# Two more blocks of h, dg and du loaded through transposing DMAs, gram's sums copied out by ScalarE, and shift_k's gradient stored unturned

## The chip, the cores and the metric

The kernel runs on one core of a Trainium2 chip. The core has five engines, each with its own queue of instructions that run in order: TensorE (PE in the profile, its weight loads shown apart as PEld), VectorE (DVE), ScalarE (ACT), GpSimd (POOL), and SyncE (SP), which here does nothing but issue DMAs. Engines wait for one another on semaphores. [...] Sixteen DMA engines, fed by rings that are filled from the queues of SP and ScalarE, carry everything between HBM and SBUF. The metric is device time in microseconds (us), the median over runs.

## The reference

The computation is the forward pass and all gradients of a sum of two branches on a layernormed input. S = 2048 rows, D = 512 channels, F = 1376 hidden units, all in bf16.

```
xn = layernorm(q)
A:  k_shift = causal convolution of k with shift_k (4 taps per channel)
    kv  = k_shift * v
    y   = causal convolution of kv with ssm_k over all S rows (by FFT) + kv * ssm_D
    out_A = xn * y
B:  h = (xn @ w_gate) * (xn @ w_up);  out_B = h @ w_down
out = q + out_A + out_B
outputs: out, and the gradients of q, k, v, shift_k, ssm_k, ssm_D, w_gate, w_up, w_down
```

The gradients that matter below: those of w_gate, w_up and w_down are products over all 2048 rows, xn^T dg, xn^T du and h^T grad_out, for which h, dg and du must lie with rows on partitions. The gradient of shift_k, 512 x 4 numbers, is for each channel and tap a sum over rows of k (shifted) times the gradient of k_shift.

## The kernel before, in words

The work has three stages. In the first (to about 117 us) the layernorm, the tables of the FFT and the first transforms are done. In the second (to about 300 us) the loop over eight chunks of 256 rows computes the gate, up and down products with hidden units on partitions, multiplies them to h, dg and du, and writes the first seven chunks of those to HBM (HDD); between them the groups of the FFT are worked off. The eighth chunk's h, dg, du stay in SBUF (hd).

The third stage (from 300 us to the end) is where the change lies. Its backbone is `dw`, a loop over the 11 blocks of 128 hidden units (the last has 96). For block fb it runs `down_grad` (16 products, line L1026, into pd: the gradient of w_down) and then 64 products (L1062, into pu: the gradients of w_gate and w_up, in two halves). Both need block fb's h, dg and du with rows on partitions, and there are two ways to get them:

- Blocks 0 to 6: `load_hb` loads the block as it lies (hb, one plain DMA of 1344 KB, L793), and `hid_t` turns it on TensorE, 16 transposes for each of h, dg and du (L859, into pt); ScalarE copies each set of 16 out of PSUM (128x2048, the helper line L235). h and dg are turned before the previous block's L1062 products, du in the middle of the previous block's `down_grad`.
- Blocks 7 to 10 (`TURNED`): `load_t` loads them with a DMA that transposes on the way (natT, L817), and only the eighth chunk, which is in SBUF, is turned on TensorE by `last_t` (six transposes, L829). Block 9 (`SPLIT`) is loaded into two tiles by two DMAs, of five chunks and of two.

The buffers are few: `hb` and `natd` have two each, `nath` one. So the load for block fb + 2 waits until TensorE is through with an older block. `behind(fb)` puts some transposing loads behind a named DMA in SP's order.

Beside the backbone, generators are called at fixed steps of the loop (`sides`): `inv_y` (inverse transforms, four row groups; loads vb and kb, multiplies on VectorE into dks at L962 and kb at L963, at last loads khC), `ew` (alternating `final` and `bwd`, the elementwise work on VectorE: `final` waits for a load bb of 512 KB, L1127, at its line L1139, and needs an output buffer that an earlier output DMA must have left, L1138), `dsk_gram` and `inv_dk` (products po, L1001; outputs o5t).

`dsk_gram` makes shift_k's gradient: for each of four groups of 128 channels 32 products of dks with khC (L1085, into the PSUM tile pk), of which only the diagonal of each 64x64 square is wanted. VectorE multiplies pk by the identity straight out of PSUM (L1091, two 64x256 instructions) and sums along the row (L1093). At the end a cast to bf16 (L1096), four transposes on TensorE (L1101) and a copy out of PSUM by VectorE (dskt) turn the result so that it is stored in rows of 1 KB (L1104). ssm_D's gradient dDt is likewise turned and copied out by VectorE (L1019).

A scheduler sets the order of each engine's queue from the order of the program and its own estimates; `tc.high_priority` pulls instructions forward, `tc.issue_after` holds one behind another in its queue. SP's DMAs go out strictly in order, so a DMA that waits for its data, its buffer or a lane holds back all behind it.

Of the kernel before, what the change touches and what calls it, by code (L numbers as in the profile page):

```python
# [8 lines left out]
BF = mybir.dt.bfloat16  # L9
F32 = mybir.dt.float32  # L10
I32 = mybir.dt.int32
ALU = mybir.AluOpType
ACTF = mybir.ActivationFunctionType
AX = mybir.AxisListType
# [6 lines left out]
R = 16  # L21
P = 128
NC4 = 4
FBLK = [(i * 128, min(128, F - i * 128)) for i in range((F + 127) // 128)]
NFB = len(FBLK)
NCH = 8
SOON = 300
# [163 lines left out]
def kernel(  # L191
# [24 lines left out]
    nc = tc.nc  # L216
# [6 lines left out]
    k_n = nat(A_k[0])  # L223
# [10 lines left out]
    def act(o, i):  # L234
        nc.scalar.copy(o, i)  # L235

    def dve(o, i):
        nc.vector.tensor_copy(o, i)  # L238
# [16 lines left out]
    def P1(name, shape, dt=F32):  # L255
        return ps1.tile(shape, dt, name=name, tag="p1")

    ident = const.tile([P, P], BF, name="ident")
# [397 lines left out]
    first = ExitStack()  # L656
# [122 lines left out]
    CP = {}  # L779
# [8 lines left out]
    LG = {}  # L788
# [6 lines left out]

    hbs = {}

    TURNED = range(NFB - 4, NFB)

    def behind(fb):  # L800
        first = {NFB - 2: lambda: LG["bb"], NFB - 1: lambda: LG["og"]}.get(fb)
        return tc.issue_after(first().ins) if first else ExitStack()

    def load_t(fb):
# [14 lines left out]
            for c in range(a, e):  # L819
                nats[fb, 0][c] = t[:, c - a]  # L820

    SPLIT = NFB - 2

    def last_t(fb):
        f0, fw = FBLK[fb]
        pt = P2("pt7", [P, 3, 2, P], BF)
        for t in range(3):
            for h in range(2):
                nc.tensor.transpose(pt[:, t, h, :fw], hds[1][:fw, fb, t, h * 128:h * 128 + 128], ident[:fw, :fw])  # L829
        n7 = c2b.tile([P, 3, 2, P], BF, name="nat7", tag="dd")  # L830
        act(n7[:, :, :, :fw], pt[:, :, :, :fw])
        nats[fb, 1] = n7

    def nat_h(fb, r):
        f0, fw = FBLK[fb]
        if fb not in TURNED:
            return nats[fb, 0][:, r, :fw]
        return nats[fb, 0][r // 2][:, 0, r % 2, :] if r < R - 2 else nats[fb, 1][:, 0, r % 2, :fw]

    def nat_d(fb, r):  # L840
        f0, fw = FBLK[fb]
        if fb not in TURNED:
            return nats[fb, 1][:, :, r, :fw]
        return nats[fb, 0][r // 2][:, 1:3, r % 2, :] if r < R - 2 else nats[fb, 1][:, 1:3, r % 2, :fw]

    def hid_t(fb, t):
        if fb in TURNED:
            return
# [68 lines left out]
    c2b = ctx.enter_context(tc.tile_pool(name="c2b", bufs=2, side="right", reuse_waits="tile"))  # L917
    c2 = ctx.enter_context(tc.tile_pool(name="c2", bufs=1, side="right", reuse_waits="tile"))
# [7 lines left out]
    dsk = c2.tile([P, NC4, 4], F32, name="dsk")  # L926
# [15 lines left out]
    DKS = {}  # L942
# [70 lines left out]
    def put_dD(o5t):  # L1013
        act(dDs[:], o5t[:, :, 0, 0])
        yield
        pt = P1("ptd", [P, P], BF)
        nc.tensor.transpose(pt[:NC4, :], dDs[:], ident[:])
        dDt = c2.tile([NC4, P], BF, name="dDt")
        dve(dDt[:], pt[:NC4, :])  # L1019
        nc.sync.dma_start(out_6.rearrange("(c p) -> c p", p=128), dDt[:])  # L1020

    def down_grad(fb):
# [18 lines left out]
    def load_h(fb):  # L1041
        (load_t if fb in TURNED else load_hb)(fb)

# [35 lines left out]
    def dsk_gram():  # L1079
        for c in range(NC4):  # L1080
            pk = P2("pk", [P, 2, D])
            for r in range(R):
                for h in range(2):
                    c0 = c * 128 + 64 * h
                    nc.tensor.matmul(pk[64 * h:64 * h + 64, h, 0:256], lhsT=dks[:, r, c0:c0 + 64],  # L1085
                                     rhs=KH[0][:, r:r + 4, c0:c0 + 64], start=(r == 0), stop=(r == R - 1))
            kd = c2b.tile([P, 4, 64], F32, name="kd", tag="dd")
            with tc.high_priority(offset=SOON):
                for h in range(2):
                    hs = slice(64 * h, 64 * h + 64)  # L1090
                    nc.vector.tensor_tensor(kd[hs], pk[hs, h, 0:256].rearrange("q (j c) -> q j c", j=4),  # L1091
                                            ident[hs, hs].unsqueeze(1).to_broadcast((64, 4, 64)), op=ALU.mult)
                nc.vector.tensor_reduce(dsk[:, c, :], kd[:], axis=AX.X, op=ALU.add)  # L1093
            yield
        dskb = c2.tile([P, 4, NC4], BF, name="dskb")
        nc.vector.tensor_copy(dskb[:], dsk[:].rearrange("q c i -> q i c"))  # L1096
        for _ in range(2):
            yield
        pt = P1("pts", [P, 4, P], BF)
        for j in range(4):  # L1100
            nc.tensor.transpose(pt[:NC4, j, :], dskb[:, 3 - j, :], ident[:])  # L1101
        dskt = c2b.tile([NC4, P, 4], BF, name="dskt", tag="dd")
        dve(dskt[:], pt[:NC4].rearrange("c j q -> c q j"))
        nc.sync.dma_start(out_4.rearrange("(c p) j -> c p j", p=128), dskt[:])  # L1104
        yield

    def bwd(b):
# [15 lines left out]
    late = []  # L1123
# [35 lines left out]
    def load_kh():  # L1159
        khC = c2.tile([P, R + 3, D], BF, name="khC", tag="o5k")  # L1160
        nc.gpsimd.memset(khC[0:1, 0:3, :], 0.0)
        with tc.issue_after(LG["g"].ins):
            nc.sync.dma_start(khC[:, 3:3 + R, :], k_n)
            nc.sync.dma_start(khC[1:113, 0:3, :], k_n[0:112, R - 3:R, :])
            nc.sync.dma_start(khC[113:128, 0:3, :], k_n[112:127, R - 3:R, :])
        KH.append(khC)

    def every(gen, start, step):
# [8 lines left out]

    def put_late():
        for dst, t in late:
            nc.sync.dma_start(dst, t[:])  # L1180
        late.clear()

    def ew():
# [55 lines left out]
```

## Time and profile before

| | |
|---|---|
| median of 3 runs | 480.36 us (480.18 to 481.91) |
| the profiled execution | 481.82 us, of which span 480.0 us |
| TensorE busy | 464.5 us, 97% |
| VectorE busy | 340.5 us, 71% (80.57 of the last 97 us) |
| ScalarE busy | 305.6 us, 64% (33.02 of the last 97 us) |
| DMA | 139.85 MB, mean 291 GB/s; 96% of the rings' time in the last 97 us |

A timeline row reads: start in us from the span's start, length in us, engine, line, operation, output <- inputs, shapes, count, and in brackets the idle time of that engine just before, with what ended it. "SPq" is the DMA-issuing queue of SP. Matmuls are pipelined, so the length of a row of several runs a little beyond the start of the next; start to start is the time that they take on TensorE. In the DMA view the figures after "x1" of an issue are its size and the time from issue to landing; its slices are fortieths of the window asked for.

### The profile page before, as it was taken

What the parts mean: (1) busy time and instruction counts of PE and PEld (TensorE: products, weight loads), DVE (VectorE), ACT (ScalarE), POOL (GpSimd) and SP (SyncE); (2) the same over time, 40 slices, a digit from 0 to 9 for tenths busy, and PEclk for the clock granted to TensorE, in tenths of its full rate; (3) what the DMA queues carried; (4) which work ended last, traced back from release to release, by engine and by line L of the source; (5) the groups of instructions that cost most, each with busy time, mean ns of one, the idle gap of its engine ahead of it and who ended that gap; (6) DMA issues with size and microseconds to landing.
All of it is one profiled execution on the core that took longest, in us unless ns stands there. A gap on an engine that the chain in (4) does not pass through costs nothing.

```text
span 480.0 us, 10366 instructions
## 1 busy us (share of the span) xinstructions
PE 464.5 (97%) x4252; PEld 311.6 (65%) x4293; DVE 340.5 (71%) x609; ACT 305.6 (64%) x349; POOL 14.0 (3%) x30
## 2 busy tenths in 40 slices
PE   7999999999999999999999999999999999999996
PEld 6867755547648447447447743576777687677885
DVE  7889989979366567686777877022257899599893
ACT  4957677659568678779779975375576535233141
POOL 8000000000000000000000000110000000000000
PEclk9999999999999999999999999999999999999999
DMA  8999999989998968968978379999899979999858
GB/s 268 374 381 366 310 296 320 315 300 328 318 288 270 277 202 255 285 200 245 298 235 259 118 272 331 388 329 313 312 361 364 371 260 320 318 267 239 252 155 294
DMA packets 111132, 139.85 MB, mean 291 GB/s; under 512 B 38859, under 2 KB 84336, under 8 KB 109550
## 3 DMA queue, kind: packets, MB, share of 16 engines
q1 hardware_dynamic: 109502, 137.85, 89.7%
q10 hardware_dynamic: 1584, 1.36, 1.0%
q8 instruction: 33, 0.54, 0.5%
q14 instruction: 13, 0.11, 0.1%
HBM read 67.08 MB, written 63.41 MB: 272 GB/s over the span
## 4 chain that ended last, share of the span: by engine, by line
PE 67%; DMA 15%; DVE 14%; issue 2%; SPq 2%; ACT 1%; DVEq 0%; ACTq 0%
PE px L555 15%; PE pgu L512 13%; PE pu L1062 8%; PE py L548 7%; PE pdh L518 6%; PE pd L1026 4%; PE ps L584 3%; DMA khC<-in_A_k_dram 3%; PE pg L613 3%; DMA ssk<-in_A_ssm_k_dram 2%; PE pf L370 2%; PE pt L859 2%; DMA vb<-in_A_v_dram 2%; DMA kb<-KS 2%; DMA x_b<-in_A_q_dram 2%
## 5 line engine op out<-in xcount | busy, mean ns | idle before, releaser
L555 PE MATMUL px<-WT,hd 128*128 128x512 bf16 (+1 forms) x340 | 78.6, 379 | 1.6 <-issue 1.4
L1062 PEld LDWEIGHTS <-xnC 128*128 128x128 bf16 x704 | 67.0, 98 | 8.4 <-issue 0.6
L555 PEld LDWEIGHTS <-hd 128*128 128x128 bf16 (+1 forms) x352 | 32.8, 98 | 44.4 <-issue 7.7
L235 ACT CAST gu<-pgu 128x1024 bf16<-128x1024 f32 (+1 forms) x48 | 45.4, 946 | 16.9 <-PE pgu L512 16.7
L235 ACT CAST GO<-pg 128x1024 bf16<-128x1024 f32 x48 | 46.2, 1015 | 13.8 <-issue 7.2
L235 ACT CAST SP<-ps 128x1024 bf16<-128x1024 f32 x47 | 45.5, 1025 | 13.7 <-PE ps L584 11.8
L512 PE MATMUL pgu<-xt,Wu 128*128 128x256 bf16 (+1 forms) x352 | 53.1, 273 | 1.1 <-DVE kn L238 0.6
L600 DVE TENSOR_TENSOR T<-SP 128x2048 bf16<-128x2048 bf16 x24 | 29.3, 1222 | 34.8 <-ACT SP L235 34.7
L512 PE MATMUL pgu<-xt,Wg 128*128 128x256 bf16 (+1 forms) x352 | 52.8, 273 | 0.0
L1062 PE MATMUL pu<-natd,xnC 128*128 128x256 bf16 x448 | 51.2, 273 | 0.0
L518 PE MATMUL pdh<-gt,WdT 128*128 128x256 bf16 (+1 forms) x352 | 46.9, 273 | 0.1
L235 ACT CAST fst<-pf 128x1024 bf16<-128x1024 f32 x44 | 42.7, 1031 | 5.5 <-issue 2.3
L512 PEld LDWEIGHTS <-Wu 128*128 128x128 bf16 (+1 forms) x352 | 33.0, 100 | 15.6 <-issue 10.7
L548 PE MATMUL py<-Wd,hd 128*128 128x512 bf16 (+1 forms) x167 | 40.2, 379 | 0.8 <-issue 0.5
L235 ACT CAST og<-pu 128x1024 bf16<-128x1024 f32 (+1 forms) x11 | 10.9, 993 | 43.7 <-PE pu L1062 28.3
L518 PEld LDWEIGHTS <-WdT 128*128 128x128 bf16 (+1 forms) x352 | 34.9, 100 | 4.8
L512 PEld LDWEIGHTS <-Wg 128*128 128x128 bf16 (+1 forms) x352 | 34.8, 100 | 3.7
L235 ACT COPY natd<-pt 128x2048 bf16<-128x2048 bf16 x14 | 26.2, 1875 | 12.0 <-PE pt L859 12.0
L533 DVE TENSOR_TENSOR hd<-gu,dh 128x1024 bf16<-128x1024 bf16 (+1 forms) x48 | 30.8, 641 | 0.8
L532 DVE TENSOR_TENSOR hd<-gu 128x512 bf16<-128x512 bf16 (+1 forms) x48 | 19.0, 397 | 16.7 <-ACT gu L235 16.7
L548 PEld LDWEIGHTS <-hd 128*128 128x128 bf16 (+1 forms) x176 | 16.5, 98 | 20.8 <-issue 3.1
L600 DVE TENSOR_TENSOR U<-SP 128x2048 bf16<-128x2048 bf16 x24 | 29.2, 1218 | 0.0
(177 smaller groups left out, 687.4 us busy)
## 6 DMA issues: line engine op xcount, KB each, us to landing
HDD<-hd SPq DMA_DIRECT2D x35, 384.0 KB, 4.5
FD<-fst SPq DMA_DIRECT2D x24, 512.0 KB, 4.9
X<-FD SPq DMA_DIRECT2D x24, 512.0 KB, 5.5
GD<-GO SPq DMA_DIRECT2D x24, 512.0 KB, 3.9
g<-GD SPq DMA_DIRECT2D x11, 1024.0 KB, 8.9
hb<-HDD SPq DMA_DIRECT2D x7, 1344.0 KB, 10.2
bb<-BX SPq DMA_DIRECT2D x8, 512.0 KB, 5.5
BX<-bx SPq DMA_DIRECT2D x7, 512.0 KB, 3.9
```

What stands on the lines that cost most here:

```text
L235: nc.scalar.copy(o, i)
L512: nc.tensor.matmul(pgu[:w, i, t, :], lhsT=W[:, c, f0:f0 + w], rhs=xt[:, :, c, :], start=(c == 0), stop=(c == NC4 - 1))
L518: nc.tensor.matmul(pdh[:w, i, :], lhsT=WdT[:, c, f0:f0 + w], rhs=gt[:, :, c, :], start=(c == 0), stop=(c == NC4 - 1))
L532: nc.vector.tensor_tensor(hd[:fw, fb0:fb0 + n, 0, :], gu[:fw, :n, 0, :], gu[:fw, :n, 1, :], op=ALU.mult)
L533: nc.vector.tensor_tensor(hd[:fw, fb0:fb0 + n, 1:3, :], gu[:fw, :n], dh[:fw, :n].unsqueeze(2).to_broadcast((fw, n, 2, 256)), op=ALU.mult)
L548: nc.tensor.matmul(py[:], lhsT=hd[:fw, fb, 0, ss], rhs=Wd[:fw, fb, :], start=(fb == 0), stop=(fb == NFB - 1))
L555: nc.tensor.matmul(px[:], lhsT=hd[:fw, fb, t, ss], rhs=W[:fw, fb, :], start=(t == 1 and fb == 0), stop=(t == 2 and fb == NFB - 1))
L584: nc.tensor.matmul(ps[32 * q:32 * q + 32, a, :], lhsT=TB.EF[64 * a:64 * a + 64, 4 * g + q, ri].rearrange("p k j -> p (k j)"), rhs=X[64 * a ...
L600: tt(W[:].rearrange("p c a d -> p c (a d)"), A[:, i:i + 1].rearrange("p c a d -> p c (a d)").to_broadcast((P, 2, 2 * D)), B[:].rearrange(" ...
L613: nc.tensor.matmul(pg[q // 2][64 * a:64 * a + 64, q % 2, :], lhsT=TB.EI[32 * q:32 * q + 32, 2 * g + a, yi].rearrange("p k c -> p (k c)"), ...
L1026: nc.tensor.matmul(pd[:fw, :], lhsT=nat_h(fb, r), rhs=goC[:, r, :], start=(r == 0), stop=(r == R - 1))
L1062: nc.tensor.matmul(pu[:, c, :, :fw], lhsT=xnC[:, r, cs(c)], rhs=nat_d(fb, r), start=(r == 0), stop=(r == R - 1))
```

## The change

- `TURNED` grows from the last four blocks to the last six: blocks 5 and 6 are now loaded by transposing DMAs, and only their eighth chunk is turned on TensorE. Their plain loads, their 96 transposes and six copies of 128x2048 are gone; twelve transposes and two copies of 128x768 are added.
- The split load is now that of block 7 (the eighth); block 9 is loaded whole. The eighth chunk of the first turned block goes to a `natd` buffer.
- `behind` now names a DMA for each turned block: block 5's load comes after the last load of khC (`LG["kh"]`), block 6's after the last kb load of `inv_y`, block 7's after the last g load issued, block 8's after ssm_k's last g loads, 9 and 10 as before after bb and og.
- In `dsk_gram` ScalarE first copies each 64x256 half of pk to SBUF (kd), and VectorE multiplies there; kd now holds two groups, and these VectorE instructions lose their high priority.
- shift_k's gradient is no longer turned: four small VectorE copies put it into the order of the output, and one DMA stores it with 8 bytes a row, issued after an output of `put_late`. The four transposes and the copy dskt are gone.
- dDt is copied out by ScalarE instead of VectorE.

```diff
-    TURNED = range(NFB - 4, NFB)
+    TURNED = range(NFB - 6, NFB)

     def behind(fb):
-        first = {NFB - 2: lambda: LG["bb"], NFB - 1: lambda: LG["og"]}.get(fb)
+        first = {NFB - 6: lambda: LG["kh"], NFB - 5: lambda: DKS["kb", R - 2], NFB - 4: lambda: LG["g"], NFB - 3: lambda: LG["gk"], NFB - 2: lambda: LG["bb"], NFB - 1: lambda: LG["og"]}.get(fb)
         return tc.issue_after(first().ins) if first else ExitStack()
...
-    SPLIT = NFB - 2
+    SPLIT = NFB - 4
...
-        n7 = c2b.tile([P, 3, 2, P], BF, name="nat7", tag="dd")
+        n7 = CP["n"].tile([P, 3, 2, P], BF, name="nat7", tag="natd", bufs=2) if fb == TURNED[0] else c2b.tile([P, 3, 2, P], BF, name="nat7", tag="dd")
...
-        dve(dDt[:], pt[:NC4, :])
+        act(dDt[:], pt[:NC4, :])
...
-            kd = c2b.tile([P, 4, 64], F32, name="kd", tag="dd")
-            with tc.high_priority(offset=SOON):
-                for h in range(2):
-                    hs = slice(64 * h, 64 * h + 64)
-                    nc.vector.tensor_tensor(kd[hs], pk[hs, h, 0:256].rearrange("q (j c) -> q j c", j=4),
-                                            ident[hs, hs].unsqueeze(1).to_broadcast((64, 4, 64)), op=ALU.mult)
-                nc.vector.tensor_reduce(dsk[:, c, :], kd[:], axis=AX.X, op=ALU.add)
+            if c % 2 == 0:
+                kd = c2b.tile([P, 2, 4, 64], F32, name="kd", tag="dd")
+            for h in range(2):
+                hs = slice(64 * h, 64 * h + 64)
+                act(kd[hs, c % 2], pk[hs, h, 0:256].rearrange("q (j c) -> q j c", j=4))
+                nc.vector.tensor_tensor(kd[hs, c % 2], kd[hs, c % 2], ident[hs, hs].unsqueeze(1).to_broadcast((64, 4, 64)), op=ALU.mult)
+            nc.vector.tensor_reduce(dsk[:, c, :], kd[:, c % 2], axis=AX.X, op=ALU.add)
             yield
-        dskb = c2.tile([P, 4, NC4], BF, name="dskb")
-        nc.vector.tensor_copy(dskb[:], dsk[:].rearrange("q c i -> q i c"))
-        for _ in range(2):
+        dskb = c2.tile([P, NC4, 4], BF, name="dskb")
+        for j in range(4):
+            nc.vector.tensor_copy(dskb[:, :, j], dsk[:, :, 3 - j])
+        for _ in range(4):
             yield
-        pt = P1("pts", [P, 4, P], BF)
-        for j in range(4):
-            nc.tensor.transpose(pt[:NC4, j, :], dskb[:, 3 - j, :], ident[:])
-        dskt = c2b.tile([NC4, P, 4], BF, name="dskt", tag="dd")
-        dve(dskt[:], pt[:NC4].rearrange("c j q -> c q j"))
-        nc.sync.dma_start(out_4.rearrange("(c p) j -> c p j", p=128), dskt[:])
+        with tc.issue_after(LG["late"].ins), nc.allow_non_contiguous_dma(reason="2 KB of shift_k's gradient, 8 bytes a row"):
+            nc.sync.dma_start(out_4.rearrange("(c p) j -> p c j", p=128), dskb[:])
         yield
...
-            nc.sync.dma_start(khC[113:128, 0:3, :], k_n[112:127, R - 3:R, :])
+            LG["kh"] = nc.sync.dma_start(khC[113:128, 0:3, :], k_n[112:127, R - 3:R, :])
...
-            nc.sync.dma_start(dst, t[:])
+            LG["late"] = nc.sync.dma_start(dst, t[:])
```

## The prediction, made before the changed kernel was run

> **What bounds the kernel now.** I read the page's busy shares first, then its slices, then the last 120 us engine by engine (timelines of TensorE, VectorE and the SP queue, then the DMA view of single windows). Line numbers are those of the kernel before; blocks are counted 0 to 10.
>
> ```profile
> PE 464.5 (97%) x4252; PEld 311.6 (65%) x4293; DVE 340.5 (71%) x609; ACT 305.6 (64%) x349; POOL 14.0 (3%) x30
> ...
> DVE  7889989979366567686777877022257899599893
> ...
> DMA  8999999989998968968978379999899979999858
> ```
>
> TensorE is the bound: 97% busy, at full clock. But from slice 31 on (372 us) VectorE is nearly full too, and the DMA rings are eight or nine tenths busy from 288 to 444 us save for one slice. Only that last stretch is touched. In it the TensorE timeline shows work back to back, with these transposes of blocks 5 and 6 in it:
>
> ```profile
> 381.78 1.67 PE L1026 MATMUL pd<-goC,nath 128*128 128x512 bf16 x7
> 383.61 0.96 PE L859 MATMUL pt<-ident,hb 128*128 128x128 bf16 x14 [0.16 <-DMA hb<-HDD]
> ...
> 385.41 3.66 PE L1062 MATMUL pu<-natd,xnC 128*128 128x256 bf16 x32
> ...
> 417.64 0.95 PE L859 MATMUL pt<-ident,hb 128*128 128x128 bf16 x14 [1.06 <-DVE kd L1091]
> ```
>
> VectorE's timeline shows where it waits in the same stretch; it ends at 471.76, and TensorE at 475.84:
>
> ```profile
> 380.42 0.69 DVE L1139 TENSOR_TENSOR o<-o,bb 128x1024 bf16<-128x1024 bf16 x1 [0.64 <-DMA bb<-BX]
> ...
> 387.85 0.69 DVE L962 TENSOR_TENSOR dks<-dd,vb 128x1024 bf16<-128x1024 bf16 x1
> ...
> 413.62 0.69 DVE L1138 TENSOR_TENSOR o<-xnC,yC 128x1024 bf16<-128x1024 bf16 x1 [4.29 <-DMA out_dram<-o]
> ...
> 416.00 0.69 DVE L1139 TENSOR_TENSOR o<-o,bb 128x1024 bf16<-128x1024 bf16 x1 [1.09 <-DMA bb<-BX]
> ```
>
> The SP queue issues in order, and a transposing load holds it for 9 to 10 us where a plain one takes half a microsecond. The DMA view of the window 420.45 to 429.4 shows what the second does to the rings: 40 slices of 0.22 us, a gap of nearly nothing, then a steady 290 GB/s.
>
> ```profile
> 368.24 0.49 SPq L793 DMA_DIRECT2D hb<-HDD  x1
> ...
> 399.05 9.69 SPq L817 DMA_TRANSPOSE natT<-HDD  x1
> ```
>
> ```profile
> GB/s 364 359 387 357 341 330 339 325 343 309 359 368 359 385 322 294 245 171 132 121 37 192 222 9 0 2 8 9 10 193 292 288 287 292 292 288 292 292 289 286
> ...
> natT<-HDD SPq DMA_TRANSPOSE x1, 11.1
> ```
>
> **TensorE, removed and added.** Measured from start to start, blocks 5 and 6 lose 48 transposes each: the first two thirds of block 5 from 383.29 (381.78 plus seven products at 0.215) to 385.41, 2.12 us; its last third 398.07 to 398.96, 0.89; the first two thirds of block 6 400.69 to 402.96, 2.27, a wait for the gram multiply in it; its last third 416.42 to 418.55, 2.13, of which 1.06 is such a wait. The four transposes of shift_k's gradient go: 424.75 to 425.07, 0.32. Sum 7.73. Added: six transposes for the last chunk of each block (L829; 425.07 to 425.41 shows 0.33), 0.66. Net 7.1 us less, all on the path, since TensorE is back to back there.
>
> **First giveback: block 5's load.** The order of the changed program puts the first product of block 5 (L1026, one) straight after block 4's last, and every later TensorE instruction is behind it. So TensorE stands at 383.3 until the transposing load has landed. That load goes out right behind the three of khC (issued by 366.1; the last landed 12.7 us after 365.48, at 378.1). Its buffer is free by then (block 3's last transposes end at 365.2). How long from the landing of what is ahead in the rings to its own landing is read from the two whole ones: 406.0 to 413.0, 7.0; 425.5 to 431.5, 6.0. So it lands at 384.1 to 385.1: a wait of 0.8 to 1.8, I take 1.3.
>
> **Second giveback: the gram.** On SP, behind that load, lie two outputs, bb of the third `final`, an od output and the vb and kb loads; on the rings they come after it. In the first such load's wake, bb landed (416.0) 3.0 us after it with three outputs of 256 KB between, some 0.6 each; here two: bb at 384.6 + 2.3 = 386.9, against 380.3 before. VectorE reaches the last dks product from there in 3.7 us (L1139 0.6, two L1146 1.22, L962, L963 and L962 1.9; the new order has them ahead of the rest of `final`): 390.6. TensorE begins the first gram group at 384.6 + 0.2 + 3.5 = 388.3, and only the last four of its 32 products need those rows: 28 at 0.0585 is 389.95. Wait 0.65. After that group TensorE stands where it stood before (390.87), with 5.1 us of the saving still ahead.
>
> **The second load and the others.** Block 6's load can start at 385.2 (its queue lane needs the first to land), holds SP to 394.5 and lands by 397; block 6 needs it at some 411. Queued behind it on SP: two outputs, two kb, a dk, bb of the fourth `final` (397.2 instead of 389.55, landing 401), og. VectorE, 1 to 3 us later than before by then, gets to that bb at 402.6, so it hardly waits. The og copy on ScalarE waits for og's outputs until 403 (before: 396.3), and od and the third gram copy stand behind it; the PSUM buffer it frees is wanted at 405.2. Cover of 1 to 2 us, thin. Blocks 7 to 10 are loaded at 400, 420, 432 and 446 and are needed 5 to 10 us after they land; if that cover goes, TensorE pays one for one.
>
> **VectorE.** It starts the third `final` 6.5 us later. Its three later waits, 4.29 + 1.09 + 1.68 (the last at 447.01) = 7.06, all for outputs and bb held back by transposing loads, go: those loads now come earlier against VectorE's own work. Work: dskt 0.68 and dDt 0.20 go, four dskb copies of 0.16 (row of L1096: 0.168) replace one; the eight gram multiplies keep at most their 0.42 and at least 0.34 (half of L1147's 0.684), so 0 to 0.6 less; I take 0, since their width is unchanged. Net 0.4 less. End: 471.76 + 6.5 - 7.06 - 0.4 = 470.8, only 1.0 earlier.
>
> **ScalarE and the rest.** Six copies of 1.88 go; two of 0.80, dDt's 0.20 and eight gram copies come, each between 0.37 (od, 96x256) and 0.59 (od, 128x512): 5 us less in all, on an engine idle for 64 of the last 97 us; cost 0 unless the og wait above holds it. shift_k's output of 512 pieces of 8 bytes: issue from 0.29 (its predecessor) up; the two og outputs, 1024 pieces, landed in 5.3, so under 5; nobody waits for it but a queue lane of the last load, which has 10 us to spare. Cost 0; the bound above is 2 us of ring time in a stretch where VectorE has 2 us of cover.
>
> **Sum.** TensorE: 7.1 - 1.3 - 0.65 = 5.1 us earlier. VectorE ends at 470.8; behind its last dk output SP still issues og1 twice and od. That took from 472.98 to 476.73 before, 3.75 us behind a megabyte of o5t; without that load, 1.3. So od goes out at 472.1 to 474.6 where TensorE alone would allow 471.6: 4.6 to 2.2 earlier. The o5t outputs now leave some 2 us before, so I go near the quick end: 4.2 us. The profiled execution: span 480.0, itself 481.82, 1.46 over the median of 480.36. 481.82 - 4.2 = 477.6; against the median, 476.2.
>
> [...] The trace's own rates are 290 GB/s for a transposing load behind a gap of 1.4 us, and 404 to 416 GB/s in windows of plain loads (396 to 398, 378 to 382). [...]
>
> **Rivals.**
> 1. Full gain. Block 5's load is already queued when the rings get to it, so it may pass at hb's pace: 1344 KB in 3.4 us. Landing 382, bb 384, the dks rows 388, no TensorE wait, VectorE ends at 468: 7.1 less, 473.3. Against it: a load issued 5 us ahead of its turn (399.05, turn at 404) still showed the gap. 0.2.
> 2. Slower: VectorE becomes the end. It is 6.5 us late at 386.9 and keeps its 7.06 of waits, because each bb and each output buffer still comes behind a load that holds SP. End 471.76 + 6.5 - 0.4 = 477.9, od out between 479.2 and 481.6, 2.5 to 4.9 later: 482.9 to 485.3, say 484. It decides once more than 4.5 of the 7.06 stay. For it: each of its three waits stood behind such a load. 0.14.
> 3. Most of the gain lost: block 5's load lands at 387 to 388 (13.9 us issue to landing is the longest yet, and the rings are fullest here), or og's wait reaches the PSUM buffers. 3 to 4 us more given back: 479.5. 0.16.
>
> The forecast has 0.5, with its own range 474.3 to 478. A change under 0.5% (2.4 us) could hardly be told from none. Faster: the forecast, rival 1 and a little of 3, 0.70; same 0.15; slower 0.15. The range leaves out the far ends: 472.8 to 481.5.
>
> **What will show it.** Right: SP held some 10 us or more from 366; VectorE's L1139 on bb near 387; a wait at the first product on natT near 383.3 and one late in the first gram group; block 7's down product starting near 424 instead of 428.9; no VectorE wait over 1 us after 405; TensorE and VectorE ending within 1 us of each other. Wrong: natT landing before 383 (then rival 1), or VectorE's old waits still there at 410 to 450 (rival 2), or ScalarE's og wait followed by an idle TensorE (rival 3).

## The result

The changed kernel took 485.04 us (median of 10 runs), the kernel before 480.27 on the same chip: ratio 1.0097, 95% interval 1.0076 to 1.0119. It is 4.8 us slower, where 4.2 less was forecast; the range (472.8 to 481.5) does not hold it. The profiled execution of the changed kernel took 485.67, its span is 483.9.

### The profile page after: what moved, and what is told of

The parts are those of the page before. It is cut to its first block, busy times and chain, and to the rows that moved or that the text cites. A ratio compares the mean times of both kernels' runs of the same rounds, so it can differ in the third digit from the quotient of the medians.

```text
span 483.9 us, 10195 instructions
## 1 busy us (share of the span) xinstructions
PE 462.5 (96%) x4164; PEld 308.2 (64%) x4205; DVE 339.4 (70%) x610; ACT 298.9 (62%) x354; POOL 13.9 (3%) x30
## 4 chain that ended last, share of the span: by engine, by line
PE 65%; DVE 15%; DMA 15%; issue 2%; ACT 2%; SPq 1%; ACTq 0%; DVEq 0%
PE px L555 13%; PE pgu L512 13%; PE pu L1062 9%; PE py L548 7%; PE pdh L518 6%; PE pd L1026 4%; PE pq L932 3%; PE ps L584 3%; PE pg L613 3%; PE pt L859 3%; DMA ssk<-in_A_ssm_k_dram 2%; PE pf L370 2%; DMA bb<-BX 2%; DMA out_dram<-og 2%; DMA hb<-HDD 2%
## 5 line engine op out<-in xcount | busy, mean ns | idle before, releaser
L1062 PEld LDWEIGHTS <-xnC 128*128 128x128 bf16 x704 | 68.0, 99 | 14.7 <-issue 6.0
L1062 PE MATMUL pu<-natT,xnC 128*128 128x256 bf16 (+1 forms) x336 | 40.6, 274 | 5.4 <-ACT og L235 5.4
L1062 PE MATMUL pu<-natd,xnC 128*128 128x256 bf16 x320 | 36.6, 273 | 0.0
```

The lines of the kernel that those rows point to most:

```text
L1062: nc.tensor.matmul(pu[:, c, :, :fw], lhsT=xnC[:, r, cs(c)], rhs=nat_d(fb, r), start=(r == 0), stop=(r == R - 1))
```

## The profile after

The lines of the page that answer to those shown of before (busy times, then slices of 12.1 us):

```profile
PE 462.5 (96%) x4164; PEld 308.2 (64%) x4205; DVE 339.4 (70%) x610; ACT 298.9 (62%) x354; POOL 13.9 (3%) x30
...
PEclk9999999999999999999999999999999999999989
DMA  9999999989997969878977299999999999999986
```

TensorE has 88 products and transposes fewer, as meant, yet the span is longer. The granted clock has an 8 in the last slice but one (460 to 472 us), where it was full before. Line numbers of the changed kernel are three lower than before's from L1104 on, so L1136 is the old L1139.

The first half of the stretch went near the forecast. SP's queue (start, length of the issue) and then TensorE's timeline:

```profile
366.71 14.18 SPq L817 DMA_TRANSPOSE natT<-HDD  x1
...
385.18 9.44 SPq L817 DMA_TRANSPOSE natT<-HDD  x1
```

```profile
383.99 0.38 PE L1026 MATMUL pd<-goC,natT 128*128 128x512 bf16 x1
...
389.91 0.41 PE L1085 MATMUL pk<-khC,dks 128*64 128x256 bf16 x4 [0.45 <-DVE dks L962]
391.12 0.41 PE L1085 MATMUL pk<-khC,dks 128*64 128x256 bf16 x4 [0.79 <-DVE dks L962]
...
424.55 2.97 PE L1026 MATMUL pd<-goC,natT 128*128 128x512 bf16 x13
...
441.81 1.07 PE L1001 MATMUL po<-IW,g 128*128 128x128 bf16 x16 [1.04 <-DMA g<-GD]
...
460.82 3.14 PE L1062 MATMUL pu<-natT,xnC 128*128 128x256 bf16 x14 [5.39 <-ACT og L235]
```

SP is held 14.2 us from 366.7. The first product on natT starts without a wait, two waits of 1.24 in all stand in the first gram group, and block 7's down product starts at 424.55, 4.4 earlier than in the profile of before (2.2 earlier than in a second profile of that kernel, f3 below). Then that lead is lost: 1.04 for a g load, 5.39 for og, and 14 products after it take 3.14 us where 1.69 is usual. VectorE's timeline again shows waits for outputs and for bb:

```profile
383.75 0.69 DVE L1135 TENSOR_TENSOR o<-xnC,yC 128x1024 bf16<-128x1024 bf16 x1 [5.88 <-DMA out_dram<-o]
...
387.34 0.69 DVE L1136 TENSOR_TENSOR o<-o,bb 128x1024 bf16<-128x1024 bf16 x1 [2.27 <-DMA bb<-BX]
...
421.65 0.69 DVE L1136 TENSOR_TENSOR o<-o,bb 128x1024 bf16<-128x1024 bf16 x1 [2.26 <-DMA bb<-BX]
...
455.26 0.69 DVE L1135 TENSOR_TENSOR o<-xnC,yC 128x1024 bf16<-128x1024 bf16 x1 [4.10 <-DMA out_dram<-o]
```

What lies behind 460.82 is in the chain that ended last (start, length, what):

```profile
450.57 0.41 SPq L1073
...
451.04 8.63 DMA out_dram<-og
...
459.76 1.02 ACT og L235
...
460.82 5.33 PE pu L1062 x32
```

og has one buffer. The second output of blocks 6 and 7 took 8.6 us to land, ScalarE could not copy block 8's sums until then, and so TensorE could not begin block 9's. Why it took so long is in the DMA view of the window 446.5 to 455.5, 40 slices of 0.225 us:

```profile
GB/s 353 272 50 6 1 8 9 10 66 288 291 291 328 405 64 410 410 173 27 27 0 0 0 0 9 0 9 0 55 46 0 18 200 255 255 282 328 360 346 392
...
out_dram<-dskb SPq DMA_DIRECT2D x1, 4.0 KB, 7.4
```

The first gap (447.2 to 448.5) is the usual one around a transposing load (1.4 us in the kernel before). The second, 450.5 to 453.7, is new. It comes half a microsecond behind the 512 pieces of 8 bytes of shift_k's gradient, which themselves took 9 ns each and were done by 450. Of the 2048-byte packets behind them fifteen, begun between 450.38 and 450.45, took 2.0 to 3.3 us each, where 0.08 is usual, and most of the few that began after 452 took 0.6 to 1.8. The store, issued at 447.15, landed at 454.60, 7.4 us later.

## The experiments

Theory S: the unturned store stalls the rings, and its gap is the loss. Theory L: the two extra transposing loads make the outputs late. Ratios are to the kernel before, run beside each on the same chip (medians 479.3 to 479.8). Executions of one kernel spread over some 4 us, so an interval of the ratio is 0.1 to 0.4% wide on each side. A ratio is formed over all executions and can differ from the quotient of the two medians by up to 0.16%. Most runs have ten executions or more; e6 and e12 have four, e9 eight, f3 one. Differences between runs are of medians that were taken on different chips; where it matters the difference by the ratios stands beside it.

### Taking the change apart

**e1, the store turned as before.**

```diff
...
-            nc.sync.dma_start(out_4.rearrange("(c p) j -> p c j", p=128), dskb[:])
+        pt = P1("pts", [P, 4, P], BF)
+        for j in range(4):
+            nc.tensor.transpose(pt[:NC4, j, :], dskb[:, 3 - j, :], ident[:])
+        dskt = c2b.tile([NC4, P, 4], BF, name="dskt", tag="dd")
+        dve(dskt[:], pt[:NC4].rearrange("c j q -> c q j"))
+        nc.sync.dma_start(out_4.rearrange("(c p) j -> c p j", p=128), dskt[:])
```

> The changed kernel with shift_k's gradient turned and stored as before (four transposes on TensorE, dskt by VectorE, rows of 1 KB); all else as changed. Theory S (the 512 pieces of 8 bytes stall the DMA rings for some 4 us at 450, og's outputs land late, and TensorE waits 5.4 us for the PSUM bank behind ScalarE's og copy and then runs its next 32 products 1.6 us slower): no gap in the rings at the store, ScalarE's longest og wait 4 to 6 us instead of 12.2, no TensorE wait over 1.5 us after 440, no VectorE wait of 4 us at L1138; time 477 to 480, that is 5 to 8 below the changed kernel. Theory L (the two more transposing loads hold SP and the rings, so outputs land late whatever the store is): the og wait stays at 10 us or more, time 484 to 486.

Measured: 481.81, ratio 1.0032 (1.0007 to 1.0057). 3.2 of the loss go with the store, but the time lies between the two theories. TensorE's timeline of this run has a wait that the changed kernel has not, for VectorE's late copy out of PSUM:

```profile
431.85 0.22 PE L1017 MATMUL ptd<-ident,dDs 128*4 128x128 bf16 x1 [3.07 <-DVE dskt L238]
```

**e2, the store alone:** the kernel before with the unturned store; loads, gram and dDt as before.

```diff
...
-        for j in range(4):
-            nc.tensor.transpose(pt[:NC4, j, :], dskb[:, 3 - j, :], ident[:])
...
-        nc.sync.dma_start(out_4.rearrange("(c p) j -> c p j", p=128), dskt[:])
+        with tc.issue_after(LG["late"].ins), nc.allow_non_contiguous_dma(...):
+            nc.sync.dma_start(out_4.rearrange("(c p) j -> p c j", p=128), dskb[:])
```

> The kernel before with the store alone changed (four small VectorE copies, 512 pieces of 8 bytes, no transposes on TensorE); loads and gram copies as before. Theory S: the rings show the same gap of about 4 us behind that store, at some 433 to 447; what lands behind it comes 4 us late; time 1 to 5 over before, according to what is just behind it. Theory L: no gap, time within 1 of before, rather 0.3 less for the four transposes.

Measured: 480.70, ratio 1.0020 (0.9999 to 1.0042): some 1 us, 2 at most by the interval. The gap is there (444.7 to 446.8, under 30 GB/s; the store landed after 5.5 us), but og's outputs go out at 450.2 in this kernel, behind it, and TensorE has no wait over 0.5 us from 366 on. So the gap costs little here; what it costs depends on what stands right behind it.

**e3, the same store in 128 pieces of 32 bytes** (side by side as well, two to each 64 bytes; shift_k's gradient comes out in another order of rows).

```diff
-            nc.sync.dma_start(out_4.rearrange("(c p) j -> p c j", p=128), dskb[:])
+            nc.sync.dma_start(out_4.rearrange("(p c) j -> p (c j)", p=128), dskb[:].rearrange("p c j -> p (c j)"))
```

> The changed kernel with the same 4 KB stored in 128 pieces of 32 bytes, one per partition, so that the rows of shift_k's gradient are out of order; all else as changed. Theory S, cost by the number of pieces: a gap a quarter as long, about 1 us, time 478 to 481. Theory S, cost by any piece smaller than some line: the gap stays near 4 us, time 484 to 486. Theory L: time 484 to 486, with no gap to be seen at the store.

Measured: 479.52, ratio 1.0009 (0.9985 to 1.0034), 5.5 under the changed kernel. The DMA view of the window 445.5 to 454.5 has only the first gap, and the store landed in 3.3 us:

```profile
GB/s 291 357 273 207 31 0 2 8 10 9 179 290 289 364 321 439 419 346 428 419 405 373 410 455 182 146 182 200 237 182 473 346 307 278 325 341 346 341 344 287
...
out_dram<-dskb SPq DMA_DIRECT2D x1, 4.0 KB, 3.3
```

Theory S holds, for 5.5 us by the medians and 4.2 by the ratios. But TensorE still has two of its waits, so the loads do not bring what was forecast even without the gap:

```profile
440.99 1.07 PE L1001 MATMUL po<-IW,g 128*128 128x128 bf16 x16 [1.26 <-DMA g<-GD]
...
456.73 1.69 PE L1062 MATMUL pu<-natT,xnC 128*128 128x256 bf16 x14 [2.11 <-ACT og L235]
```

**e5, the loads alone** (the kernel before with the new `TURNED`, `SPLIT`, `behind` and the buffer of `last_t`; gram, the store and dDt as before).

> The kernel before with the loads alone changed (blocks 5 and 6 by transposing loads, block 7 split, the order of the loads); gram's multiply straight from PSUM, store and dDt as before. Theory S: as the first of these runs to within 1 us, 477 to 480, so 0 to 3 below before: of TensorE's 7.1 us some 4.4 were left at block 7 (424.55 against 428.91), and VectorE, late by 7 us at 387, sets how much of it reaches the end. Theory L: 484 to 486.

Measured: 480.25, ratio 1.0017 (0.9992 to 1.0042): no gain, no loss. TensorE waits 2.84 us for dskt, as in e1.

### What in the store is dear

**e11 and e16, the 8-byte pieces in the same place of the queue, but 512 and 64 bytes apart** in a scratch tensor; the output itself follows later in pieces of 32 bytes.

```diff
+    BX, DS = ..., dram.tile([P, 4, 256], BF, name="DS")      # e16: [P, 4, 32]
...
-            nc.sync.dma_start(out_4.rearrange("(c p) j -> p c j", p=128), dskb[:])
+            nc.sync.dma_start(DS[:, :, 0:4], dskb[:])
+        for _ in range(5):
+            yield
+        with tc.issue_after(LG["late"].ins):
+            nc.sync.dma_start(out_4.rearrange("(p c) j -> p (c j)", p=128), dskb[:].rearrange("p c j -> p (c j)"))
```

> The changed kernel, with the 512 pieces of 8 bytes written at the same place in SP's queue, but to a scratch area where each lies 512 bytes from the next; the real output is written some 15 to 25 us later in 128 pieces of 32 bytes (rows out of order). Theory L (the pieces are dear because eight of them, from different partitions, share each 64 bytes of the target): no gap of over 1 us at the store, which lands within 4 us; the og wait shrinks to 1 to 3 us; 479 to 481. Theory N (it is the number of pieces, wherever they go): the gap of 4 us and the 7 us landing stay, as does TensorE's wait of 5 us: 485 to 487.

> As the run with the 8-byte pieces 512 bytes apart in a scratch area (480.2; the store landed 3.8 us after its issue, no gap), with the pieces 64 bytes apart. Theory L (eight pieces in the same 64 bytes are what is dear): again no gap, landing within 4.5 us, 479.5 to 481. Theory M (neighbours within 512 bytes already hinder one another): a gap of 1 to 4 us after the store's packets, landing in 5 to 7.5 us, 481.5 to 485.

Measured: 480.24 (ratio 1.0014, 0.9993 to 1.0035) and 482.22 (1.0037, 1.0001 to 1.0072). The DMA views, of 445.5 to 454.5 for 512 bytes:

```profile
GB/s 347 271 53 6 0 6 9 10 84 289 289 365 308 162 428 291 392 328 373 392 423 410 410 155 46 55 182 237 273 364 403 330 316 298 310 348 346 341 323 300
...
DS<-dskb SPq DMA_DIRECT2D x1, 4.0 KB, 3.8
```

and of 446.5 to 455.5 for 64 bytes:

```profile
GB/s 290 354 273 157 20 0 5 9 9 10 258 290 290 364 274 214 382 400 191 73 291 382 391 396 382 237 355 237 200 182 273 218 364 314 344 321 328 348 346 332
...
DS<-dskb SPq DMA_DIRECT2D x1, 4.0 KB, 4.2
```

As many pieces of 8 bytes, in the same place of the queue, land in 3.8 and 4.2 us and leave no second gap when each has 64 bytes to itself (the fall to 46 and 55 GB/s in e11 lasts half a microsecond). So the number of pieces is not the price, and being side by side is not by itself either, since e3's pieces of 32 bytes are (3.3 us to landing, no second gap): what the changed kernel's store has and these have not is eight pieces from eight partitions written into the same 64 bytes, with 7.4 us to landing and a second gap of 3.2. Two things are not shown: which spacing between 8 and 64 bytes would do, and whether packed 8-byte pieces stall in a scratch tensor too, since e11 and e16 changed the target along with the spacing. e16's time lies 2 us above e11's, where theory M had put it, but with neither theory M's gap nor its landing time. The intervals overlap, the two profiles have the same og wait (2.6 and 2.8 us), and the rest stays open.

**e8, the packed store issued by ScalarE.**

```diff
-        with tc.issue_after(LG["late"].ins), nc.allow_non_contiguous_dma(...):
-            nc.sync.dma_start(out_4.rearrange("(c p) j -> p c j", p=128), dskb[:])
+        with nc.allow_non_contiguous_dma(...):
+            nc.scalar.dma_start(out_4.rearrange("(c p) j -> p c j", p=128), dskb[:])
```

> The changed kernel, with the store of shift_k's gradient in 512 pieces of 8 bytes issued from ScalarE's queue, ahead of the og copy of block 6 (near 430 instead of 447 us), and SP without it. Theory A (the pieces stall all the rings, whoever issues them): the GB/s line shows the same gap of some 4 us, now near 430 to 435, where a transposing load and g loads are under way; og's outputs at 450 are free of it; 479 to 482. Theory B (only SP's own ring stands behind the pieces): no gap in the GB/s line, the store lands late but nothing else does; 478 to 480, as with the store in 32-byte pieces (479.5).

Measured: 483.12, ratio 1.0076 (1.0049 to 1.0103). Neither theory's time came, and neither was tested cleanly. The store stood ahead of the og copy in ScalarE's queue and waited there 9.4 us for VectorE's dskb; TensorE lost 3.44 at 419 through it. What the trace does show speaks for theory B: the store was issued at 417.6 and landed only after 8.9 us, but in no slice from 416 to 427 do the rings stop, though they are slower, with 91 to 320 GB/s, from 421.2 on. It is one store at another time, so this is not settled.

### Why the loads do not pay

**e6, og's outputs of blocks 4 to 7 issued by ScalarE.**

```diff
-        first = {..., NFB - 1: lambda: LG["og"]}.get(fb)
+        first = {..., NFB - 1: lambda: LG["bb"]}.get(fb)
...
-                    LG["og"] = nc.sync.dma_start(o[:, a:f0 + fw]...
+                    LG["og"] = (nc.scalar if fb in (5, 7) else nc.sync).dma_start(o[:, a:f0 + fw]...
```

> The changed kernel, with the outputs og of the block pairs 4-5 and 6-7 issued from ScalarE's queue, right behind ScalarE's own copy, instead of from SP; the last transposing load is placed behind bb instead of behind og, and nothing else is moved. In the changed kernel those of blocks 6-7 were ready near 441.5 us and issued by SP only at 450.6, behind a transposing load, od and the store of shift_k's gradient; the single og buffer then kept ScalarE 12.2 us and TensorE 5.4 us. Theory Q (what the early loads gain is lost where og's outputs stand in SP's queue; the stall of the small store counts only because og stands behind it): issued near 442, landed by 452, ScalarE's wait for og under 4, TensorE's wait on og gone and the 1.6 of slower products behind it too: 485.0 less 7, 477 to 479. Rival R (the rings are full in the last 100 us, so every byte that goes earlier pushes another later): a wait of the same size comes back elsewhere on TensorE or VectorE, 483 to 486.

Measured: 488.08, ratio 1.0176 (1.0133 to 1.0218), the worst of all. Theory Q predicted the opposite, and even rival R no more than 486. The first output of blocks 6 and 7 went out at 441.73, nine us earlier, but the second had to wait on ScalarE for the landing of the transposing load (450.55), and every copy behind it waited too. ScalarE's timeline:

```profile
450.99 1.01 ACT L235 CAST o5t<-po 128x1024 bf16<-128x1024 f32 x1 [14.35 <-DMA natT<-HDD]
```

Here (14.35 us) and in e8 (9.43) a DMA issued by ScalarE brought its waits into ScalarE's own queue. So og's place in the order was not tried cleanly by this run; the last transposing load, whose named DMA had been og, also went behind bb instead.

**e12 and e13, a second buffer for og** (blocks 8 and 9 in the space that nath leaves free), in the changed kernel and in e3. Every queue keeps its order.

```diff
-            og = ... else c2.tile([P, 2, NC4, 2 * P], BF, name="og")
+            og = ... else CP["n"].tile([P, 2, NC4, 2 * P], BF, name="og", tag="nath") if fb == 8 else c2.tile(...)
```

> The changed kernel, with og of the last full pair of blocks (8 and 9) in the buffer that nath leaves free after block 7, instead of in the one og buffer; every queue keeps its order, instruction by instruction. ScalarE's copy for block 8 then waits for no output. In the changed kernel's trace that wait was 12.2 us on ScalarE and 5.4 on TensorE, with 1.6 more of slower products behind it. Theory T (TensorE's wait is what sets the end): TensorE ends 7 us earlier, 472.5, and the time is 477 to 479. Theory V (VectorE, itself held by the outputs behind the store's gap, ends at 477.3 whatever og does, and its last output sets the end): TensorE's og wait goes as in T, but the time falls by only 2 to 3: 482 to 483. Rival R (the rings are full; the wait comes back on TensorE under another name): 484 or more, with a new TensorE wait of 4 us.

> As the run with the store in 128 pieces of 32 bytes (rows of shift_k's gradient out of order; 479.5), with og of blocks 8 and 9 in nath's buffer as well. There TensorE waited 2.1 us for og and ended at 473.8, VectorE at 472.6. Theory T: 2.1 less, 477.2 to 477.8. Theory V: VectorE's end at 472.6 is next, so only about 1 less, 478 to 479, and its two waits of 9 us for outputs and 4 for bb remain. Rival R: 479.5 again, another wait in og's place.

Measured: 482.31 (ratio 1.0063, 1.0042 to 1.0084) and 480.04 (1.0008, 0.9989 to 1.0028). TensorE's large og wait is gone in both. In e12 TensorE ends at 470.98, 8.5 us earlier than in the changed kernel (7.2 when the start of the execution is taken out, as in the table below), and the time falls by 2.7 only (1.6 by the ratios): VectorE's last dk is at 474.89, as theory V said. In e13 nothing is gained over e3, as rival R said; TensorE's wait for the g load is 1.97 there.

**e9, bb and two outputs ahead of block 5's load.**

```diff
-        first = {NFB - 6: lambda: LG["kh"], ...
+        first = {NFB - 6: lambda: LG["bb"], ...
```

> The changed kernel, with block 5's transposing load behind the third bb in SP's queue (so two outputs and bb go out at 366 instead of 381). Theory V (VectorE, 7 us late at the third final's bb, is what the rest of the stretch runs behind: its late copies and outputs hold SP, the rings and ScalarE later): bb lands by 380, VectorE's chain is 6 to 7 us earlier up to 400, the block 5 load lands 2 to 3 us later (386 to 387, TensorE waits 2 to 3 there), the later waits for outputs and og shrink by more: 480 to 482.5. Theory Q (VectorE's lateness is beside the point): TensorE's 2 to 3 us come on top, the 5.4 us og wait stays: 486 to 488.

Measured: 483.64, ratio 1.0075 (1.0045 to 1.0106), 1.4 under the changed kernel (1.1 by the ratios), between the two theories. VectorE's third `final` starts at 378.9 instead of 387.3, TensorE waits 0.7 for natT, and yet VectorE ends only 2.4 earlier and og still costs 5.16. So VectorE's late start is a small part.

**e14 and e15, the parts put together:** turned store with dskt by ScalarE and og's second buffer; e15 has also bb ahead of block 5's load.

> The changed kernel with shift_k's gradient turned on TensorE as before, its copy out of PSUM (dskt) by ScalarE instead of VectorE, and og of blocks 8 and 9 in nath's buffer. The run with the turned store had 481.8, with a TensorE wait of 3.1 us for VectorE's late dskt copy and 0.6 for og. Theory V: the 3.1 goes, 478 to 479.5, and VectorE (ended at 474.2 there, 0.9 of its work gone now) is the last. Theory T: 477.5 to 478.5. Rival R (the loads' gain can't reach the end at all): 480.5 to 482.

> As the run with the turned store, dskt by ScalarE and og's second buffer, and in addition the third bb and two outputs ahead of block 5's transposing load. Theory V (VectorE's lateness of 7 us from 387 on is what is left): VectorE ends 2 to 3 us earlier, TensorE pays 0.7 at the first product of block 5: 1 to 2 under the run without it, 476.5 to 478. Theory T: 0.7 over it.

Measured: 479.09 (ratio 1.0005, 0.9983 to 1.0027) and 479.87 (1.0017, 0.9994 to 1.0040). e14 lies where theory V put it; e15 is 0.8 over e14, as theory T said, and not under it. With the waits for og, dskt's copy and the gap taken away (e14 has left 1.6 of TensorE's for ScalarE and 0.8 in the gram), the loads are worth nothing that can be measured. No version of the whole computation here beats the kernel before.

**f3, the kernel before once more, for a second profile.**

> The kernel before, unchanged, for a second profile. If the profiled execution used for the prediction (481.8, 1.5 over its median of then and 2.1 over the 479.7 of 31 runs) was an untypical one: the first 370 us agree within 0.7, the two waits of 1.3 us in all on the gram and VectorE's waits of 7 are smaller, and TensorE ends at 473 to 474.5 instead of 475.8. If it was typical: TensorE ends at 475 to 476.

Measured: one execution, 479.40, and TensorE ends at 473.70, not at 475.84. The profile on which the prediction rests was of an execution 2 us over the usual one, and part of what I took for the transposes' cost was that execution's waits. Rows of this second profile, to be read beside those shown of the first:

```profile
383.13 0.94 PE L859 MATMUL pt<-ident,hb 128*128 128x128 bf16 x14
...
384.02 0.94 PE L859 MATMUL pt<-ident,hb 128*128 128x128 bf16 x14
...
384.92 1.25 PE L1062 MATMUL pu<-natd,xnC 128*128 128x256 bf16 x10
...
403.95 3.67 PE L1062 MATMUL pu<-natd,xnC 128*128 128x256 bf16 x32
...
419.05 3.66 PE L1062 MATMUL pu<-natd,xnC 128*128 128x256 bf16 x32
```

A third of a block takes 0.89 (383.13, 384.02, 384.92). From 403.95 to 419.05 are 15.10 us; the first profile has 16.34 for the same work (404.83 to 421.17), with the 1.06 of a wait for the gram multiply that is not there now.

**f1, f2 and f4, less work for VectorE:** the kernel before, e14 and e12, each with half of the gradient of k left out for its last five parts.

```diff
-        for j in (0, 2):
+        for j in ((0, 2) if b < 3 else (0,)):
```

> The kernel before, with half of the gradient of k left out for the last five of its eight parts (in each the multiply of 1.23 us and two adds of 0.69 on VectorE, 13 us in all from about 420 on). Theory V (TensorE sets the end before, VectorE ends 4 us earlier and with cover): no change, 479 to 480, VectorE ends near 460. Rival: VectorE or the outputs behind it co-decide already before: 476.5 to 478.5.

> The kernel with the two loads, the turned store, dskt by ScalarE and og's second buffer (479.1), with the same 13 us of VectorE's work left out. There TensorE ended at 472.3 and VectorE at 471.9 in the profiled execution, and the last output went out behind VectorE's. Theory V: VectorE ends by 462, the outputs go out at once behind TensorE's end, 476 to 477.5, so the loads' saving comes out, 2 to 3.5 under the kernel before with the same work left out. Rival R (rings and outputs): 478.5 to 479.5.

> The changed kernel with og's second buffer (482.3; TensorE ended there at 471.0, VectorE at 474.9), with the same 13 us of VectorE's work left out. Theory V: VectorE is out of the way, the end follows TensorE: 476 to 478, though the store's gap is still there. Rival R: the gap reaches the end through the rings, 481 to 482.5.

Measured: f1 479.75 (ratio 1.0004, 0.9991 to 1.0018): VectorE, at 460.4 (11 us earlier than in the first profile, 9 than in f3), changes nothing in the kernel before. f2 478.56 (0.9984, 0.9957 to 1.0010): 1.2 under f1, the direction of theory V but not separated from nothing. f4 481.20 (1.0019, 0.9999 to 1.0040), 1.1 under e12, in the range of rival R. Its profile does not show what holds the end. TensorE starts block 2's down product at 348.24 there and at 345.16 in e12, long before anything that the edit touches, and counted from that start it ends 0.7 us earlier than in e12. What the chain of f4 does show is that the cover of the last load is used up:

```profile
447.98 6.60 DMA out_dram<-dskb
...
454.60 9.85 DMA natT<-HDD
...
464.49 5.45 PE pu L1062 x64
```

The last transposing load was issued 0.02 us after the store had landed, and it landed at 464.44. TensorE was busy with products on vb and kb until 464.38, so block 10's products began as the load landed, and TensorE lost some 0.1 us by it.

## Why the prediction was wrong

Where things ended, from the timelines of the profiled executions (us; the time of that execution in brackets). TensorE does the same work in all of them up to 383 us, yet the start of block 2's down product lies up to 1.3 us apart, so the ends are also given as counted from that start (behind the stroke):

| kernel | block 2's down product | TensorE | last dk on VectorE | span |
|---|---|---|---|---|
| before, first profile (481.82) | 345.80 | 475.84 / 130.0 | 471.77 / 126.0 | 480.0 |
| before, second, f3 (479.40) | 345.64 | 473.70 / 128.1 | 469.38 / 123.7 | 477.6 |
| changed (485.67) | 346.50 | 479.53 / 133.0 | 477.30 / 130.8 | 483.9 |
| e3, 32-byte pieces (480.66) | 345.88 | 473.76 / 127.9 | 472.59 / 126.7 | 478.9 |
| e12, og's second buffer (481.82) | 345.16 | 470.98 / 125.8 | 474.89 / 129.7 | 480.0 |
| e14, parts put together (479.46) | 346.15 | 472.31 / 126.2 | 471.90 / 125.8 | 477.7 |

**The store, "Cost 0".** This is the step that failed most. Its price was bounded by the landing time of two other outputs of 1024 pieces, "under 5", by "2 us of ring time", and by the claim that "nobody waits for it but a queue lane of the last load, which has 10 us to spare". Runs e3 and e11, stores of the same 4 KB in the same place of the queue that leave no gap, are 5.5 and 4.8 under the changed kernel (4.2 and 4.0 by the ratios). Two of the three covers failed and the third was used up. It landed in 7.4 us, not under 5. For the 2 us no row of before is named; the rings stood 3.2 us (2.1 in e2), and og's outputs, bb and the o that VectorE waits for stood behind it. And the lane (the place in the DMA queue that the last load took over from the store) held that load back: in the changed kernel it is issued at 454.62, 0.02 after the store landed, and in f4, where it is issued just as soon behind it, nothing was left of the 10 us to spare when it landed, though that cost TensorE only 0.1. The nearest row by number of pieces (og's, of 512 bytes) was not near in what mattered, how small the pieces are and where they go.

**"TensorE, removed": 7.73.** Mis-sized: in f3 a third takes 0.89, six of them 5.4, with the 0.32 of pts 5.7. Start to start in one execution had taken 2.0 of waits, marked and unmarked, into the saving. The sum was made against an execution 1.5 over the median; it took that 1.5 off at the end as an offset, but the waits that made it were in the saving.

**First and second giveback.** The places were right, the sizes together 0.7 too dear: natT cost no wait (1.3 taken), bb was there at 387.3 (386.9), the gram waits were 1.24 (0.65). Block 7's down product began at 424.55 ("near 424"), but that is in part luck: counted from block 2 the lead there is 5.0 us against the first profile, whose waits are in the saving, and 3.1 against f3.

**The og wait on ScalarE, "Cover of 1 to 2 us, thin".** The right place, the wrong instance. I followed og's wait for blocks 4 and 5 to 403, where 1 us was lost at most, and not the next one. Even without the gap it costs 2.11 (e3) to 2.83 (e16): og's outputs of blocks 6 and 7 are issued at 449.9 in e3 and 449.8 in e11, and at 449.4 in f3. SP's queue, held some 60 us by seven transposing issues (33.5 in the first profile of the kernel before, by five), did not get earlier with TensorE. TensorE only reaches this wait earlier by what it has gained. The wait for the g load (1.0 to 1.3) is of the same kind.

**VectorE, whose three later waits of 7.06 were to go.** They did not: in the changed kernel it waits 2.26 at 421 and 4.10 at 455, for a bb and an output that stood on SP behind transposing loads, the second behind the store too. Its end without the gap, 471.9 to 472.6 (e3, e11, e14), is near the 470.8 forecast, but by luck: it is 2.5 to 3.2 after f3's (2.0 to 3.3 counted from block 2), not 1.0 before.

**The sum.** For the loads without the gap, e3 against f3 on TensorE, both counted from block 2's down product: e3 is 3.5 ahead at block 7's down product, 3.7 at block 8's, 2.5 at block 9's and 0.2 at the end. Six thirds at 0.89 and the 0.32 of pts less the 0.66 added are 5.0 saved; the waits for og, g and the gram that f3 has not are 4.3 (2.11, 1.26, 0.94); the other 0.5 is not traced. Of the 7.1 that the prediction took off TensorE, then, 2.0 were waits of one execution and 4.3 went to og, g and the gram. The store's gap came on top. Both signs named for rivals 2 and 3 showed, VectorE's waits between 410 and 460 and an idle TensorE behind ScalarE's og wait. But rival 3 put only 3 to 4 us of giveback on this, and rival 2 (VectorE, 484) came near the number by luck: the store that it priced at nothing was the main cause.

That e14 takes the same time as the kernel before, although TensorE ended 1.4 earlier than in f3 (1.9 counted from block 2), fits VectorE's end (2.5 later than f3's, 2.0 counted so) and the outputs issued behind it: the last output, od, is ready at 473.16 and issued at 474.45, behind dk and og in SP's queue, where f3 issues it 0.03 after it is ready. In e3 it goes out 0.2 after it is ready, but the end comes 4.1 behind that issue instead of 3.0. f2 points to VectorE without proving it, and how much over all executions is VectorE and how much the rings stays open.

## What to carry to other kernels

Price a small store by the size of its pieces and by where they land, not by their number alone: 512 pieces of 8 bytes, eight to each 64 bytes of the target, stalled the rings for 3 us here, as many at 64 bytes' distance did not, and the stall cost what stood behind it in the same queue (8.6 us to landing for og's second output, against 5.2 in e3). Before taking work off the bound, list the things that the bound will now reach earlier (single buffers, loads, lanes) and look up when their DMAs are issued; if that time is set by an in-order queue, the saving ends there. And take a second profile of the kernel before: what is measured from start to start holds that execution's waits. Two profiles are compared from a point that the change does not touch, since their first 345 us differ by up to 3.

## What the runs showed of the hardware

**Idle time on TensorE can cost more than itself.** Behind some waits the granted clock was 0.50 to 0.54 over some 3 us. Windows of the changed kernel (columns: length, PE busy, granted clock, DMA share, GB/s), from 460 on after 5.39 us idle:

```profile
460.00:463.00 3.00, 2.17 (x11) 0.50 1.26 309
463.00:467.00 4.00, 4.00 (x36) 0.84 0.66 248
```

The window of e11 behind 2.61 us of idle time:

```profile
456.80:460.00 3.20, 3.19 (x17) 0.54 1.19 341
```

that of e3 behind 2.11:

```profile
456.60:460.00 3.40, 3.27 (x30) 1.00 1.18 338
```

and that of e1 behind 3.07:

```profile
432.00:435.00 3.00, 3.00 (x37) 1.00 1.29 299
```

The slower products cost 1.6 to 1.7 us in the changed kernel and in e11, and nothing in e1, whose idle time was longer than e11's. In f2, behind an idle time of 2.02 us, 16 products on g took 1.51 us where 1.07 is usual and the 14 after them 2.93 where 1.69 is; in e5, behind one of 2.84, the clock was 0.50 from 430 to 431. So the length of the idle time alone does not decide. What does, no run here shows.

**Block 5's transposing load, issued early, held its queue longer but landed in time.** Issued right behind khC's loads, it held SP 14.18 us (the next one 9.44), and the first product on it, at 383.99, did not wait. In this kernel the transposing loads thus mattered by when everything behind them on SP goes out, more than by when their own data come.
